# Feature work on token values kept in PSUM, in an attention and GELU kernel

## The chip, the cores and the metric

The kernel runs on one core of a Trainium2 chip. A core has TensorE (matrix products, PE in the profile, with its weight loads as PEld), VectorE (DVE), ScalarE (ACT), GpSimd (POOL) and SyncE (SP, which here only issues transfers). SBUF is the working memory, PSUM the memory that TensorE writes its products into. The metric is the device time of one execution in microseconds; before the change the median of three runs is 270.36 (270.25 to 270.38).

## What is computed

The inputs are q, k and v of 4 batches, 4 heads, 1088 tokens and 32 values each, two sketches S1 and S2 of 8 rows, and two weight matrices. In the reference, cut to what matters:

```
def phi(x):                                   # 64 features of a token
    a = einsum('rd,bhsd->bhsr', S1, x)        # 8 values
    b = einsum('rd,bhsd->bhsr', S2, x)        # 8 values
    return a (outer) b                        # 64 values
q_p, k_p = phi(q), phi(k)
kv  = k_p^T v          z = sum over tokens of k_p         # per batch and head
x   = (q_p kv) / (q_p . z + 1e-6)             # attention, 4 heads side by side: 4352 x 128
out = gelu(x @ w_in) @ w_out                  # 128 -> 2048 -> 128, exact gelu, float32
```

So every query token needs its 64 products a_i b_j, divided by its denominator, which is the sum over i, j of a_i b_j z_ij.

## The kernel before

The 4352 tokens are worked on in nine chunks: eight of 512 tokens (two for each batch, numbered 0 to 7) and one of 256 with what is left over of all batches (chunk 8). For each chunk, TensorE makes 16 hidden tiles of 128 x 512 (`hidden`, L691), ScalarE applies GELU to each (L698), GpSimd makes sums and differences of four GELU tiles at a time (`token_sums`, L741 to L744, a seven-product scheme for the second matrix), and TensorE multiplies them with w_out into two output banks (`two_products`, L776). When a chunk is done, `drain` (L788 to L797, ScalarE and VectorE) takes these two banks, `combine` (L810 to L813, VectorE) adds the parts, and `store` turns the result (L839, VectorE) and sends it out. The output banks come from a pool of two, so the next chunk's products can't begin before `drain` has read them; the buffers named "sums", which `drain` writes and `combine` and `store` read, are two as well. Chunks 0 and 1 do half of their second product in the plain way, and have one more addition in `combine` (L813).

Around this stands the attention of later chunks, on the same engines. For chunk n: `query_turn` transposes q in blocks (L535), `query_sketch` (L584) multiplies it on TensorE with a small matrix `S_abc` and leaves 16 values for each token and head in a pair of PSUM banks, a's half (4 values), c's half (4) and b (8). c is the sketch of z, folded into `S_abc`, so that the denominator is the sum of a_i c_i. `query_outer` then does everything on VectorE: it transposes the pair of banks into the SBUF tile `tok` in blocks of 32 x 32 (L595), so that a token lies in a partition, multiplies a and c (L599), sums within a partition (L601) and across to the neighbouring block of partitions, which holds the other half (L603, four instructions), adds both (L605), adds 1e-6 (L606), inverts (L607), multiplies a by it (L608), makes the outer product with b (L610, 1024 values a partition) and transposes back (L613) into `q_pT`. `attend` (L627) multiplies `q_pT` with the batch's kv on TensorE, and ScalarE copies the result to `xT` (L631), the input of `hidden`.

For keys, `finish_keys` sums kv and z of a batch on TensorE into one PSUM bank (`kv_sum`, L446: kv in columns 0 to 63, z in 64 to 127) and ScalarE copies it to `kv_T` (L470). One step later `turn_kv` turns kv on TensorE into the same bank (L475), ScalarE copies it to `kz` (L476), and `sketch_of_z` on VectorE multiplies z by the sketch (L499), reduces (L501) and writes the c part of `S_abc` (L502), which the next `query_sketch` needs. The PSUM pool `wps` has two buffers of two banks each, in turn for all of these.

The order of the work on each engine is that of the program's text: a list of steps t (one hidden tile each) with calls put at written-out steps, and a dependency from each instruction to the one before it on its engine. So an instruction that waits holds up all behind it on its engine. At step t = 32, `query_outer` of chunk 3 is written ahead of `store` of chunk 0 (t = 35) and `drain` of chunk 1 (t = 38).

Of the kernel before, what the change touches and what calls it, by code (L numbers as in the profile page):

```python
# [8 lines left out]
FP = mybir.dt.float32  # L9
U32 = mybir.dt.uint32  # L10
AX = mybir.AluOpType
# [5 lines left out]
def kernel(  # L17
# [18 lines left out]
    pe, dve, act, pool, sp = nc.tensor, nc.vector, nc.scalar, nc.gpsimd, nc.sync  # L36
    B, H, S, D = q.shape
    R = S1.shape[0]
    F = R * R
# [3 lines left out]
    NP = H // 2  # L43
# [4 lines left out]
    CW = JC * 128  # L48
# [12 lines left out]
    att = ctx.enter_context(tc.tile_pool(name="att", bufs=2))  # L61
# [5 lines left out]
    def work_banks():  # L67

        return wps.tile([128, 2, CW], FP, name="w_ps")

    def work_bank():
        return work_banks()[:, 0]
# [7 lines left out]
    def out_bank():  # L80
        return ops.tile([128, CW], FP, name="o_ps")
# [133 lines left out]
    ident = big.tile([128, 128], FP, name="ident")  # L215
# [8 lines left out]
    kz = [big.tile([128, 128], FP, name=f"kz{b}") for b in range(B)]  # L224
# [81 lines left out]
    sT = big.tile([128, 2 * R], FP, name="sT")  # L306
# [119 lines left out]
    def flat(features):  # L426
        return features.rearrange("p i j -> p (i j)")
# [16 lines left out]
    def kv_product(ps, lhsT, features, h, part, start=False, stop=False):  # L444

        pe.matmul(ps[h * D:(h + 1) * D, part * F:(part + 1) * F], lhsT=lhsT, rhs=features, start=start, stop=stop,  # L446
                  skip_group_check=True)

    def kv_sum(b, ps):


        for i in range(J):
            ch, t, one = i % 2, i // 4, i // 2 % 2
            for h in range(H):
                kv_product(ps, main["v", b][:, h, i, :], flat(k_p[b, h % 2][:, t, h // 2 * 4 + ch * 2 + one]), h, 0,
                           start=i == 0)
        for h in range(H):
            kv_product(ps, v_rem_aug[b][:, h, :], flat(k_p_rem[b % 2][:, h]), h, 0, stop=True)
        if b == 1:
            for h in range(H):  # L460
                kv_product(ps, ones_rem, flat(k_p_rem[b][:, h]), h, 1)
        for m in range(2 if b == 1 else 1):
            for h in range(H):
                kv_product(ps, ones, k_s[h % 2][:, h // 2, 0, m], h, 1, stop=b > 1 or m == 1)

    kv_T = {}

    def take_kv(b, ps):
        kv_T[b] = att.tile([128, 128], FP, name="kv_T")
        act.copy(out=kv_T[b], in_=ps[:, :128])  # L470

    def turn_kv(b, ps):

        for rows in (slice(0, 64), slice(64, 128)):
            pe.matmul(ps[rows, :128], lhsT=kv_T[b][:, :F], rhs=ident, start=True, stop=True)  # L475
        act.copy(out=kz[b], in_=ps[:, :128])  # L476
        sketch_of_z(b, kv_T[b][:, F:])


    S_abc = [big.tile([128, 2, 2, 2 * R], FP, name=f"S_abc{b}") for b in range(B)]  # L480
# [12 lines left out]
        for b in range(1, B):  # L493
            pool.tensor_copy(out=S_abc[b], in_=w)

    def sketch_of_z(b, z):

        zs = att.tile([128, R, R], FP, name="z_s")
        dve.tensor_mul(out=zs, in0=z.rearrange("p (i j) -> p i j", i=R), in1=sT[:, None, R:].broadcast_to([128, R, R]))  # L499
        c = att.tile([128, R], FP, name="c_s")  # L500
        dve.tensor_reduce(out=c, in_=zs, axis=mybir.AxisListType.X, op=AX.add)  # L501
        dve.tensor_mul(out=S_abc[b][:, :, :, 4:8], in0=c.rearrange("p (i f) -> p i f", i=2)[:, :, None].broadcast_to([128, 2, 2, 4]),  # L502
                       in1=own_r[:, None, :, None].broadcast_to([128, 2, 2, 4]))
# [11 lines left out]
    def turn_first_kv():  # L515

        ps, zs = work_bank(), held["zs"]
        for h in range(H):
            c, r = h // 2, h % 2
            pe.matmul(ps[h * D:(h + 1) * D, :F], lhsT=zs[:, r], rhs=ident[:, c * F:(c + 1) * F], start=True, stop=True)  # L520
        sketch_of_z(0, ps[:, :F])


    qT, qp, xT = {}, {}, {}
# [46 lines left out]
    sketched = {}  # L571
# [18 lines left out]
    def query_outer(n):  # L590

        W = width[n]
        K = W // 16
        tok = att.tile([128, 2, CW // 2], FP, name="A_sb").rearrange("p i x -> p (i x)")
        dve.transpose(out=tok[:, :W].rearrange("p (c x) -> p c x", c=NP), in_=sketched.pop(n)[:, :, :W // 2])  # L595
        x = tok[:, :W].rearrange("p (k x) -> p k x", x=2 * R)
        a, c, b = x[:, :, 0:4], x[:, :, 4:8], x[:, :, 8:16]
        m = att.tile([128, 32, 4], FP, name="q_ac")[:, :K]
        dve.tensor_mul(out=m, in0=a, in1=c)  # L599
        part, other = (att.tile([128, 32], FP, name=f"q_den{i}")[:, :K] for i in range(2))  # L600
        dve.tensor_reduce(out=part, in_=m, axis=mybir.AxisListType.X, op=AX.add)  # L601
        for g in range(4):
            dve.tensor_reduce(out=other[(g ^ 1) * 32:((g ^ 1) + 1) * 32], in_=m[g * 32:(g + 1) * 32], axis=mybir.AxisListType.X,  # L603
                              op=AX.add)
        dve.tensor_add(out=part, in0=part, in1=other)  # L605
        dve.tensor_scalar(out=part, in0=part, scalar1=1e-6, scalar2=None, op0=AX.add)  # L606
        dve.reciprocal(out=part, in_=part)  # L607
        dve.tensor_mul(out=m, in0=a, in1=part[:, :, None].broadcast_to([128, K, 4]))  # L608
        feat = att.tile([128, 2 * CW], FP, name="q_f", bufs=1)[:, :2 * W]
        dve.tensor_mul(out=feat.rearrange("p (k i j) -> p k i j", i=4, j=R), in0=m[:, :, :, None].broadcast_to([128, K, 4, R]),  # L610
                       in1=b[:, :, None, :].broadcast_to([128, K, 4, R]))
        qp[n] = att.tile([128, 2, CW], FP, name="q_pT")
        dve.transpose(out=qp[n].rearrange("f r x -> f (r x)")[:, :2 * W], in_=feat)  # L613

    def attend(n):
# [259 lines left out]
    banks = [out_bank(), out_bank()]  # L875
# [86 lines left out]
    held = {}  # L962
# [6 lines left out]
        key_features_rem(pair, held["rem"])  # L969

    def finish_keys(b):
        held["kv"] = work_bank()
        kv_sum(b, held["kv"])
        take_kv(b, held["kv"])

    def round_at(t, w, product_by=dve):
        r = []
# [18 lines left out]
    at(18, channel_sums, 4)  # L996

    at(21, finish_keys, 1)
    at(22, lambda: turn_kv(1, held["kv"]))
    at(23, query_turn, 3)  # L1000
    at(23, query_sketch, 2)
    at(23, query_outer, 2)
    at(29, attend, 2)
    for i, t in enumerate((25, 26, 28)):
        at(t, channel_sums, i)
    at(11, spread_sketches)
    at(40, repeat_first_z)
    at(46, turn_first_kv)
    for n in range(3, NCHUNK):

        t = (n - 1) * NF
        b = (n + 1) // 2
        keys = n % 2 and b < B
        if n > 3:
            at(t - 6, query_turn, n)
        at(t, query_sketch, n)
        at(t, query_outer, n)
        if keys:
            for r in range(2):
                at(t - 2, key_turn_blocks, b, r)  # L1020

        at(t + 7, attend, n)
        if keys:
            at(t + 5 + (n == NCH + 1), features_of_all, b)
            at(t + 5 + (n == NCH + 1), outer_of_all, b)
            at(t + 6, add_last, b, dve)
            at(t + 8, widen_v_rem, b)
            at(t + 14, finish_keys, b)
            at(t + 15, lambda b=b: turn_kv(b, held["kv"]))
# [5 lines left out]
    for t, (n, fi) in enumerate(steps):  # L1035
# [13 lines left out]
        elif fi % NB == NB - 1:  # L1049
            b = fi // NB  # L1050
# [11 lines left out]
    for t in range(len(steps) + LAG):  # L1062
        if t < 4:
# [9 lines left out]
            if t == 3:  # L1073
                banks = work_banks()
# [17 lines left out]
        if t < len(steps):  # L1092
            n, fi = steps[t]
            hidden(n, fi, by_halves=t >= 18 and (n < NMAIN or fi < 5))
        if t < len(steps) and steps[t][0] < NMAIN and steps[t][1] % NB == NB - 1:
            n, b = steps[t][0], steps[t][1] // NB
# [50 lines left out]
```

## Time and profile before

| what | us |
|---|---|
| median of 3 runs | 270.36 |
| span of the profiled run | 270.7 |
| TensorE busy | 262.9 (97%) |
| GpSimd busy | 177.9 (66%) |
| VectorE busy | 158.4 (58%) |
| ScalarE busy | 118.0 (44%) |

VectorE's groups that the diff touches, by line, with the mean of the full-width instructions and, from the timelines, the shortest and longest of those looked at:

| line | what | count | mean ns | from, to us |
|---|---|---|---|---|
| L595 | transpose out of PSUM | 6 | 709 | 0.67, 0.72 |
| L599 | a times c | 6 | 709 | 0.29, 1.27 |
| L605 | add both halves | 6 | 448 | 0.19, 0.96 |
| L606 | add 1e-6 | 6 | 555 | 0.18, 1.31 |
| L608 | a divided | 6 | 545 | 0.29, 1.05 |
| L610 | outer product | 6 | 1579 | 1.22, 2.36 |
| L613 | transpose back | 6 | 1245 | 1.25, 1.25 |
| L499 | z times sketch, from `kv_T` | 3 | 479 | 0.21, 0.74 |
| L502 | c part of `S_abc` | 4 | 604 | 0.17, 1.22 |

How to read it: the page gives shares over the whole span; a row of 40 digits gives the busy tenths of each fortieth of the span (6.8 us), and the row of the clock the granted TensorE clock in tenths. A timeline's line gives start and duration in us, the engine, the line of the kernel, the operation, output and inputs, and in brackets the idle time before it and what ended that. Equal instructions of very different durations, as in the last column, were held up by something while they ran.

### The profile page before, as it was taken

To read this page: it belongs to the slowest core of one execution; us is meant where nothing else is said; L and a number is where in the kernel's file an instruction comes from. 1 tells how busy PE (TensorE), PEld (TensorE's weight loads), DVE (VectorE), ACT (ScalarE), POOL (GpSimd) and SP (SyncE) were. 2 spreads that over 40 slices of the span, in tenths; PEclk is the share of its full clock that TensorE was granted. 3 is DMA by queue.
4 is the path that set the end of the run, shared out by engine and by line. 5 is a ranking of instruction groups with operands and counts; after the bars stand their busy time and mean duration, and the time that the engine had idled before them with its cause. 6 is when DMAs were issued, how large, how long until landed. Compare 5 with 4: busy or idle time off the path is not lost.

```text
span 270.7 us, 6127 instructions
## 1 busy us (share of the span) xinstructions
PE 262.9 (97%) x2489; PEld 135.7 (50%) x2489; DVE 158.4 (58%) x308; ACT 118.0 (44%) x239; POOL 177.9 (66%) x180
## 2 busy tenths in 40 slices
PE   8999999999999599999999999999999999999995
PEld 6755444355344255444445455544454444445794
DVE  2687778469599897577048992870097107600140
ACT  4464767433633333353336333353326333534431
POOL 3423006899999568597777776786879687868400
PEclk9999999999999799999999999999999999999999
DMA  6459363444300110101100002002000200020021
GB/s 202 126 151 368 89 175 63 115 120 125 86 10 2 23 19 14 27 2 22 17 2 2 1 0 41 2 1 39 2 0 2 40 2 0 2 39 0 2 32 26
DMA packets 35755, 13.50 MB, mean 50 GB/s; under 512 B 28432, under 2 KB 34320, under 8 KB 35728
## 3 DMA queue, kind: packets, MB, share of 16 engines
q1 hardware_dynamic: 35536, 13.05, 19.6%
q8 instruction: 19, 0.31, 0.5%
q10 hardware_dynamic: 192, 0.07, 0.1%
q14 instruction: 8, 0.07, 0.1%
HBM read 10.88 MB, written 2.23 MB: 48 GB/s over the span
## 4 chain that ended last, share of the span: by engine, by line
PE 69%; SPq 11%; DMA 10%; DVE 7%; issue 1%; ACT 0%; POOL 0%; DVEq 0%; ACTq 0%
PE h_ps L691 31%; PE o_ps L776 28%; SPq L108 7%; DMA v<-in_v_dram 5%; DMA block<-in_moe_w_out_dram 4%; PE w_ps L824 3%; SPq L124 1%; PE w_ps L858 1%; SPq L128 1%; PE w_ps L584 1%; PE w_ps L627 1%; PE w_ps L446 1%; SPq L177 1%; DVE q_f L610 1%; PE h_ps L326 1%
## 5 line engine op out<-in xcount | busy, mean ns | idle before, releaser
L691 PE MATMUL h_ps<-xT,w_in 128*64 128x512 f32 (+3 forms) x516 | 139.5, 580 | 0.0
L698 ACT ACTIVATE block<-h_ps 128x512 f32<-128x512 f32 (+1 forms) x128 | 73.1, 571 | 121.4 <-PE h_ps L691 120.5
L776 PE MATMUL o_ps<-block,w_out 128*64 128x256 f32 x224 | 58.7, 385 | 0.0
L691 PEld LDWEIGHTS h_ps<-xT,w_in 128*64 128x64 f32 (+1 forms) x516 | 42.5, 143 | 29.1 <-issue 10.7
L741 POOL TENSOR_TENSOR bits_low<-block 128x512 f32<-128x512 f32 x28 | 39.6, 1414 | 25.0 <-ACT block L698 24.9
L776 PEld LDWEIGHTS o_ps<-block,w_out 128*64 128x64 f32 x224 | 29.8, 138 | 36.2 <-issue 25.2
L742 POOL TENSOR_TENSOR bits_a<-block 128x512 f32<-128x512 f32 x28 | 38.0, 1358 | 11.5 <-ACT block L698 11.5
L743 POOL TENSOR_TENSOR bits_e<-bits_a,block 128x512 f32<-128x512 f32 x28 | 36.9, 1316 | 2.2
L744 POOL TENSOR_TENSOR bits_m<-block,bits_e 128x512 f32<-128x512 f32 x28 | 36.3, 1297 | 2.2
L776 PE MATMUL o_ps<-block,small 128*64 128x256 f32 x112 | 29.1, 382 | 2.7 <-DVE sums L792 2.7
L595 DVE STREAM_TRANSPOSE A_sb<-w_ps 128x512 f32<-128x512 f32 (+1 forms) x7 | 4.7, 672 | 43.4 <-PE w_ps L584 43.4
L776 PE MATMUL o_ps<-bits_a,small 128*64 128x256 f32 x112 | 29.6, 388 | 0.0
L776 PE MATMUL o_ps<-bits_m,w_out 128*64 128x256 f32 x112 | 29.0, 382 | 0.0
L776 PE MATMUL o_ps<-bits_low,small 128*64 128x256 f32 x112 | 29.0, 382 | 0.0
L776 PEld LDWEIGHTS o_ps<-block,small 128*64 128x64 f32 x112 | 14.8, 137 | 22.6 <-issue 11.3
L792 DVE TENSOR_TENSOR sums<-o_ps,sums 64x512 f32<-64x512 f32 x8 | 5.5, 683 | 31.5 <-ACT sums L789 23.0
L776 PE MATMUL o_ps<-bits_e,small 128*64 128x256 f32 x112 | 17.3, 388 | 0.0
L827 PE MATMUL o_ps<-g,w_out 128*128 128x512 f32 x32 | 16.4, 599 | 0.1
L776 PEld LDWEIGHTS o_ps<-bits_a,small 128*64 128x64 f32 x112 | 15.0, 139 | 0.0
L776 PEld LDWEIGHTS o_ps<-bits_m,w_out 128*64 128x64 f32 x112 | 14.8, 137 | 0.0
L776 PEld LDWEIGHTS o_ps<-bits_low,small 128*64 128x64 f32 x112 | 14.8, 137 | 0.0
L776 PEld LDWEIGHTS o_ps<-bits_e,small 128*64 128x64 f32 x112 | 7.9, 138 | 11.3 <-issue 9.4
(187 smaller groups left out, 322.3 us busy)
## 6 DMA issues: line engine op xcount, KB each, us to landing
block<-in_moe_w_in_dram SPq DMA_DIRECT2D x3, 512.0 KB, 7.0
block<-in_moe_w_out_dram SPq DMA_DIRECT2D x3, 512.0 KB, 11.0
k<-in_k_dram SPq DMA_DIRECT2D x48, 32.0 KB, 1.8
v<-in_v_dram SPq DMA_DIRECT2D x3, 512.0 KB, 4.3
q<-in_q_dram SPq DMA_DIRECT2D x24, 64.0 KB, 3.3
out_dram<-oT SPq DMA_DIRECT2D x24, 64.0 KB, 2.2
k<-in_k_dram SPq DMA_DIRECT2D x2, 256.0 KB, 2.9
q<-in_q_dram SPq DMA_DIRECT2D x2, 256.0 KB, 4.0
```

Source lines behind the costliest of these rows:

```text
L108: sp.dma_start(out=main["k", b][pb * 32:(pb + 1) * 32, h].rearrange("t (jj jc) d -> t jj (jc d)", jj=4), in_=src[h, pb])
L595: dve.transpose(out=tok[:, :W].rearrange("p (c x) -> p c x", c=NP), in_=sketched.pop(n)[:, :, :W // 2])
L691: pe.matmul(ps[rows, :W], lhsT=w[:, rows], rhs=xT[n][:, :W], start=True, stop=True)
L698: act.activation(out=g_of[n, fi][:, :W], in_=ps[:, :W], func=ACT.Gelu)
L741: pool.tensor_sub(out=s[3], in0=a11, in1=a21)
L742: pool.tensor_add(out=s[1], in0=a21, in1=a22)
L743: pool.tensor_sub(out=s[2], in0=s[1], in1=a11)
L744: pool.tensor_sub(out=s[4], in0=a12, in1=s[2])
L776: pe.matmul(acc[n][bank][half * 64:(half + 1) * 64, col:col + HW], lhsT=fixed, rhs=moving, start=opens and e == 0 and name in "4715", stop ...
L792: dve.tensor_add(out=C[lo, 1], in0=a1[lo], in1=C[lo, 0])
L824: pe.matmul(o_of[n][i][:, :128], lhsT=g[:, i * 128:(i + 1) * 128], rhs=w_tile(w_out_sb, fi), start=first, stop=final)
L827: pe.matmul(o_of[n], lhsT=w_tile(w_out_sb, fi), rhs=g, start=first, stop=final)
```

## The change

The values of a token are no longer copied to SBUF: the transpose writes into the free halves of the same pair of PSUM banks, and a, b, c are read from there. c is copied to SBUF first, since it is multiplied with a. The two additions for the denominator become one instruction with one PSUM and one SBUF input. The outer product is two instructions, one for each bank. In `turn_kv` the pair's second bank takes the turned kv, z is read from the first bank instead of `kv_T`, and the reduced c stays in PSUM. The aim is that none of VectorE's operations in the feature work reads two operands from SBUF, the memory that GpSimd works on at the same time.

```diff
-    def turn_kv(b, ps):
+    def turn_kv(b, banks):
 
         for rows in (slice(0, 64), slice(64, 128)):
-            pe.matmul(ps[rows, :128], lhsT=kv_T[b][:, :F], rhs=ident, start=True, stop=True)
-        act.copy(out=kz[b], in_=ps[:, :128])
-        sketch_of_z(b, kv_T[b][:, F:])
+            pe.matmul(banks[rows, 1, :128], lhsT=kv_T[b][:, :F], rhs=ident, start=True, stop=True)
+        act.copy(out=kz[b], in_=banks[:, 1, :128])
+        sketch_of_z(b, banks[:, 0], F)
...
-    def sketch_of_z(b, z):
+    def sketch_of_z(b, ps, at):
 
         zs = att.tile([128, R, R], FP, name="z_s")
-        dve.tensor_mul(out=zs, in0=z.rearrange("p (i j) -> p i j", i=R), in1=sT[:, None, R:].broadcast_to([128, R, R]))
-        c = att.tile([128, R], FP, name="c_s")
+        dve.tensor_mul(out=zs, in0=ps[:, at:at + F].rearrange("p (i j) -> p i j", i=R), in1=sT[:, None, R:].broadcast_to([128, R, R]))
+        c = ps[:, 2 * F:2 * F + R]
         dve.tensor_reduce(out=c, in_=zs, axis=mybir.AxisListType.X, op=AX.add)
...
-        sketch_of_z(0, ps[:, :F])
+        sketch_of_z(0, ps, 0)
...
     def query_outer(n):
 
         W = width[n]
-        K = W // 16
-        tok = att.tile([128, 2, CW // 2], FP, name="A_sb").rearrange("p i x -> p (i x)")
-        dve.transpose(out=tok[:, :W].rearrange("p (c x) -> p c x", c=NP), in_=sketched.pop(n)[:, :, :W // 2])
-        x = tok[:, :W].rearrange("p (k x) -> p k x", x=2 * R)
-        a, c, b = x[:, :, 0:4], x[:, :, 4:8], x[:, :, 8:16]
+        K, H2 = W // 16, W // 2
+        ps = sketched.pop(n)
+        tok = ps[:, :, CW // 2:CW // 2 + H2]
+        dve.transpose(out=tok, in_=ps[:, :, :H2])
+        x = tok.rearrange("p c (k x) -> p c k x", x=2 * R)
+        a, b = x[:, :, :, 0:4], x[:, :, :, 8:16]
         m = att.tile([128, 32, 4], FP, name="q_ac")[:, :K]
-        dve.tensor_mul(out=m, in0=a, in1=c)
-        part, other = (att.tile([128, 32], FP, name=f"q_den{i}")[:, :K] for i in range(2))
+        den = att.tile([128, 32], FP, name="q_den")[:, :K]
+        by_c = lambda t: t.rearrange("p (c k) i -> p c k i", c=NP)
+        dve.tensor_copy(out=by_c(m), in_=x[:, :, :, 4:8])
+        dve.tensor_mul(out=by_c(m), in0=a, in1=by_c(m))
+        part = ps[:, 0, :K]
         dve.tensor_reduce(out=part, in_=m, axis=mybir.AxisListType.X, op=AX.add)
         for g in range(4):
-            dve.tensor_reduce(out=other[(g ^ 1) * 32:((g ^ 1) + 1) * 32], in_=m[g * 32:(g + 1) * 32], axis=mybir.AxisListType.X,
+            dve.tensor_reduce(out=den[(g ^ 1) * 32:((g ^ 1) + 1) * 32], in_=m[g * 32:(g + 1) * 32], axis=mybir.AxisListType.X,
                               op=AX.add)
-        dve.tensor_add(out=part, in0=part, in1=other)
-        dve.tensor_scalar(out=part, in0=part, scalar1=1e-6, scalar2=None, op0=AX.add)
-        dve.reciprocal(out=part, in_=part)
-        dve.tensor_mul(out=m, in0=a, in1=part[:, :, None].broadcast_to([128, K, 4]))
+        dve.scalar_tensor_tensor(out=den, in0=part, scalar=1e-6, in1=den, op0=AX.add, op1=AX.add)
+        dve.reciprocal(out=den, in_=den)
+        dve.tensor_mul(out=by_c(m), in0=a,
+                       in1=den.rearrange("p (c k) -> p c k", c=NP)[:, :, :, None].broadcast_to([128, NP, K // 2, 4]))
         feat = att.tile([128, 2 * CW], FP, name="q_f", bufs=1)[:, :2 * W]
-        dve.tensor_mul(out=feat.rearrange("p (k i j) -> p k i j", i=4, j=R), in0=m[:, :, :, None].broadcast_to([128, K, 4, R]),
-                       in1=b[:, :, None, :].broadcast_to([128, K, 4, R]))
         qp[n] = att.tile([128, 2, CW], FP, name="q_pT")
+        for c in range(NP):
+            dve.tensor_mul(out=feat[:, c * W:(c + 1) * W].rearrange("p (k i j) -> p k i j", i=4, j=R),
+                           in0=by_c(m)[:, c, :, :, None].broadcast_to([128, K // 2, 4, R]),
+                           in1=b[:, c, :, None, :].broadcast_to([128, K // 2, 4, R]))
         dve.transpose(out=qp[n].rearrange("f r x -> f (r x)")[:, :2 * W], in_=feat)
...
     def finish_keys(b):
-        held["kv"] = work_bank()
-        kv_sum(b, held["kv"])
-        take_kv(b, held["kv"])
+        held["kv"] = work_banks()
+        kv_sum(b, held["kv"][:, 0])
+        take_kv(b, held["kv"][:, 0])
```

## The prediction, made before the changed kernel ran

> **What bounds the kernel now.** I read the page first (shares, then the 40 slices), then busy time in stretches of 5 us, then the timelines of the one stretch that fell out. TensorE is the bound nearly everywhere:
>
> ```profile
> PE 262.9 (97%) x2489; PEld 135.7 (50%) x2489; DVE 158.4 (58%) x308; ACT 118.0 (44%) x239; POOL 177.9 (66%) x180
> PE   8999999999999599999999999999999999999995
> PEclk9999999999999799999999999999999999999999
> ```
>
> TensorE is idle for 270.7 - 262.9 = 7.8 us. The first 25 us and the drain of the last outputs are not touched by the change. In between there is one hole, the slice with "5", and it lies where the granted clock reads "7". The stretches (PE, PE load, DVE, ACT, POOL busy, then the clock) say the same:
>
> ```profile
> 85.00:90.00 5.00, 3.31 (x88) 1.40 (x84) 4.72 (x5) 0.69 (x2) 3.36 (x3) 1.00 0.00 0
> 90.00:95.00 5.00, 3.97 (x20) 1.89 (x22) 4.50 (x9) 2.72 (x10) 3.70 (x3) 0.70 0.21 31
> ```
>
> VectorE is busy for 4.7 and 4.5 of 5 us there. TensorE's timeline gives the hole to 10 ns, and VectorE's and ScalarE's give its cause:
>
> ```profile
> 87.65 0.66 PE L627 MATMUL w_ps<-q_pT,kz 64*32 64x256 f32 x16
> 91.03 0.43 PE L776 MATMUL o_ps<-block,small 128*64 128x256 f32 x1 [2.72 <-DVE sums L792]
> ```
>
> ```profile
> 75.83 0.67 DVE L595 STREAM_TRANSPOSE A_sb<-w_ps 128x512 f32<-128x512 f32 x1
> ...
> 78.34 0.96 DVE L605 TENSOR_TENSOR q_den<-q_den,q_den 128x32 f32<-128x32 f32 x1
> 79.34 1.31 DVE L606 TENSOR_SCALAR q_den<-q_den 128x32 f32<-128x32 f32 x1
> 80.68 0.35 DVE L607 RECIPROCAL q_den<-q_den 128x32 f32<-128x32 f32 x1
> 81.07 1.05 DVE L608 TENSOR_TENSOR q_ac<-A_sb,q_den 128x128 f32<-128x128 f32 x1
> 82.15 2.21 DVE L610 TENSOR_TENSOR q_f<-q_ac,A_sb 128x1024 f32<-128x1024 f32 x1
> 84.40 1.25 DVE L613 STREAM_TRANSPOSE q_pT<-q_f 128x1024 f32<-128x1024 f32 x1
> ...
> 89.09 0.71 DVE L839 STREAM_TRANSPOSE oT<-sums 128x512 f32<-128x512 f32 x1
> 90.30 0.68 DVE L792 TENSOR_TENSOR sums<-o_ps,sums 64x512 f32<-64x512 f32 x1 [0.49 <-ACT sums L789]
> ```
>
> ```profile
> 89.90 0.37 ACT L789 COPY sums<-o_ps 64x256 f32<-64x256 f32 x1 [1.87 <-DVE oT L839]
> ```
>
> Read it backwards. The next accumulation (L776) needs bank a1, free when L792 has read it; L792 waits for ScalarE's L789; L789 overwrites a "sums" buffer and waits for L839; L839 stands in VectorE's queue behind query_outer of chunk 3 (75.83 to 85.65) and the combine of chunk 0 (L810 to L813). So here VectorE's queue sets TensorE's time, and query_outer is 9.8 us of it. Elsewhere TensorE goes back to back, and a faster VectorE is worth nothing.
>
> The hole costs more than its 2.72 us. From 91.03 to 95.79 TensorE did sixteen products in eight pairs, four single ones (bits_e) and one hidden tile: 0.87 + 0.87 + 0.44 + 0.85 = 3.03 us by the same groups at 80.7 to 82.9. It took 4.76, and starts were 0.42 us apart instead of 0.21. So about 1.6 us of slow clock hang on the hole (0.1 I leave to restart). Together 2.72 + 1.6 = 4.3 us.
>
> [...] L605, L606, L608 took 0.96, 1.31, 1.05 us here while GpSimd ran token sums, and 0.19, 0.18, 0.29 in chunk 4 (from 114.14 us), where it paused. L606 from 79.34 to 80.65 spans GpSimd's L743, 79.33 to 80.61. [...] Here the transpose from PSUM (L595, 709 ns) is 7 ns dearer than that from SBUF (L535, 702). [...]
>
> **The change, part by part.**
> (a) query_outer. The token tile lies in PSUM, so the first product, the division product and the outer product read one PSUM and one SBUF operand. Cost from quiet rows: transpose 0.70; added copy 0.29 (as a 128x128 product); product 0.29; reduce 0.29; four reduces 1.15; one scalar-tensor-tensor for L605 and L606 0.20; reciprocal 0.35; product 0.29; outer product in two, 0.68 + 0.62 (L958, half PSUM, four in 2.46); transpose 1.25. Sum 6.1, with eleven starts at 0.03: 6.4 us. Writing PSUM from VectorE is not in the trace: [...] I take 6.7[...]. Against 9.82 in this stage that is 3.1 us less. Over seven chunks the five groups fall from 25.5 to about 16.5 us of VectorE time, all but this stage hidden behind TensorE.
> (b) Then L810, L811, L813 (two SBUF inputs, unchanged) and L839 took 4.2 us; they meet GpSimd again, so I keep it. query_outer ends at 82.5, L839 at 86.7, L789 at 87.1, L792 at 87.9, its last follower L797 2.3 later at 90.2. TensorE comes to L776 at 88.31 and to bank a0 (for L797) 0.87 + 0.44 + 0.86 later, at 90.5. So both are in time, with 0.4 and 0.3 us to spare: the hole and the slow clock go, -4.3 us.
> (c) turn_kv. z is read from PSUM, and the sketch's reduce and product write and read PSUM. That frees three small operations of GpSimd (z_s 0.74 to 0.23, S_abc 0.85 to about 0.2 at 56 us). But the built streams show that z_s now waits two ScalarE instructions later: not for the copy of kv_T (L470) but for that of kz (L476), since both banks are one tile. At batch 1:
>
> ```profile
> 56.13 0.74 DVE L499 TENSOR_TENSOR z_s<-kv_T,sT 128x64 f32<-128x64 f32 x1 [5.17 <-ACT kv_T L470]
> ```
>
> ```profile
> 57.32 0.26 ACT L476 COPY kz<-w_ps 128x128 f32<-128x128 f32 x1
> ```
>
> ```profile
> 58.13 0.67 PE L584 MATMUL w_ps<-qT,S_abc 64*32 64x256 f32 x16 [0.28 <-DVE S_abc L502]
> ```
>
> Queued behind z_s on VectorE are only its own reduce and product and the next transpose of q; the one who waits is TensorE's L584, with everything behind it. New time: kz ends 57.58, plus 0.06, z_s 0.23, reduce 0.22, product 0.20, starts 0.06, signal 0.05: 58.40, against 58.13: +0.27. At batch 2 kz ends at 109.90, so L584 may go at 110.72 instead of 110.54: +0.18. At batch 3, 167.48 and 168.12: +0.18. [...] Sum +0.6, TensorE time with nothing to hide it.
> (d) The pair of work banks is held through query_outer and the sketch instead of being free after the first transpose. With two pairs in turn the next owner of that pair is the chunk after the coming attend, and attend waits for the same query_outer anyway: nothing. The GpSimd instructions that VectorE held up become shorter (L742 at 83.24 took 2.28 against 1.30): hidden, nothing waits for them.
>
> Sum: 270.36 - 4.3 + 0.6 = 266.7; a small remainder of (b), 0.1 on average: 266.8.
>
> **Rivals.**
> 1. The chain in (b) stays a little late. For: the spare is 0.3 to 0.4[...]. Against: the 4.2 us taken already holds two such meetings. With 0.3 to 1.2 us of hole left and no slow clock, 267.1 to 268.0: say 267.6.
> 2. The waits of (c) cost nothing and the slow clock hides still more: 266.1. Against: ScalarE's kz copy ends only 0.6 us before L584, and three operations don't fit in that.
> 3. VectorE's queue is no shorter, since the PSUM forms are dear (0.4 us each on eight, which eats the 3.1)[...]. The hole stays and (c) adds 0.6: 271.0, slower. [...] Against: L958, L792 and L499 with one PSUM operand run at 0.68, 0.68 and 0.23 us, as fast as SBUF.
> 4. The hole is half closed and the slow clock stays: 270.36 - 1.36 + 0.6 = 269.6.
>
> **How the numbers follow.** Forecast 58%, rival 1 20%, rival 2 10%, rival 3 6%, rival 4 6% (a third of it within 0.2%). The time is the likeliest: 266.8. The range takes in rivals 1 and 2 and the bounds of (a) and (c): 265.8 to 268.2. Faster by over 0.2% (below 269.8): 0.92; same 0.02; slower 0.06.
>
> **What would show it.** Right: no digit under 9 in the PE and clock rows between 60 and 250 us; VectorE's operations of query_outer alike in all chunks of full width, 6.4 to 6.9 us in sum; L776 after the attend of chunk 3 with no wait; z_s released by L476, and L584 after it 0.2 to 0.3 us late three times. Wrong: a hole left near 88 us, a copy or product on PSUM well over 0.4 us, or a new hole where attend waits for q_pT.

## The result, and the profile after

The changed kernel takes 266.67 us (266.58 to 266.76, four runs) against 270.35 before (four runs on the same chip): a ratio of 0.9865, with a 95% interval of 0.9848 to 0.9882. The forecast was 266.8 us.

The page of the changed kernel has no hole left, and the clock's row is even:

```profile
PE 258.7 (98%) x2489; PEld 133.4 (50%) x2489; DVE 146.7 (55%) x315; ACT 118.0 (45%) x239; POOL 170.2 (64%) x180
...
PE   8999999999999999999999999999999999999995
...
PEclk9999999999999999999999999999999999999999
```

VectorE lost 11.7 us of busy time and GpSimd, whose code is untouched, 7.7. The same two stretches as before (PE, PE load, DVE, ACT, POOL busy, clock), and TensorE's timeline at the place of the hole:

```profile
85.00:90.00 5.00, 5.00 (x46) 2.01 (x44) 4.31 (x10) 3.59 (x12) 3.36 (x3) 1.00 0.20 31
90.00:95.00 5.00, 5.00 (x40) 2.61 (x38) 4.90 (x8) 1.22 (x3) 3.82 (x6) 1.00 0.17 26
```

```profile
85.75 0.66 PE L633 MATMUL w_ps<-q_pT,kz 64*32 64x256 f32 x16
86.37 0.43 PE L782 MATMUL o_ps<-block,small 128*64 128x256 f32 x1
```

L782 (L776 before) now follows the attend at once. VectorE's queue in the same stage (start, duration):

```profile
74.19 0.68 DVE L596 STREAM_TRANSPOSE w_ps<-w_ps 128x512 f32<-128x512 f32 x1
...
77.05 0.19 DVE L609 SCALAR_TENSOR_TENSOR q_den<-w_ps,q_den 128x32 f32<-128x32 f32 x1
77.28 0.35 DVE L610 RECIPROCAL q_den<-q_den 128x32 f32<-128x32 f32 x1
77.66 0.29 DVE L611 TENSOR_TENSOR q_ac<-w_ps,q_den 128x128 f32<-128x128 f32 x1
77.99 1.29 DVE L616 TENSOR_TENSOR q_f<-q_ac,w_ps 128x512 f32<-128x512 f32 x2
79.31 1.25 DVE L619 STREAM_TRANSPOSE q_pT<-q_f 128x1024 f32<-128x1024 f32 x1
80.48 0.81 DVE L816 TENSOR_TENSOR sums<-sums 64x256 f32<-64x256 f32 x1
81.30 1.41 DVE L817 TENSOR_TENSOR sums<-sums 64x256 f32<-64x256 f32 x1
82.75 1.65 DVE L819 TENSOR_TENSOR sums<-sums,g 128x512 f32<-128x512 f32 x1
84.43 0.71 DVE L845 STREAM_TRANSPOSE oT<-sums 128x512 f32<-128x512 f32 x1
85.63 0.68 DVE L798 TENSOR_TENSOR sums<-o_ps,sums 64x512 f32<-64x512 f32 x1 [0.49 <-ACT sums L795]
```

query_outer takes 6.37 us (74.19 to 80.56) where it took 9.82. But the reader should see the last line too: L798 ends at 86.31, and TensorE comes for its bank at 86.37. The spare time is 0.06 us; the combine (L816 to L819), with two SBUF inputs each, takes 3.9 us where it took 3.5 before:

```profile
85.56 0.38 DVE L810 TENSOR_TENSOR sums<-sums 64x256 f32<-64x256 f32 x1
85.95 1.40 DVE L811 TENSOR_TENSOR sums<-sums 64x256 f32<-64x256 f32 x1
87.39 1.67 DVE L813 TENSOR_TENSOR sums<-sums,g 128x512 f32<-128x512 f32 x1
```

The wait that the change adds, on VectorE and on TensorE (0.28 us before, 0.58 now):

```profile
55.66 0.23 DVE L499 TENSOR_TENSOR z_s<-w_ps,sT 128x64 f32<-128x64 f32 x1 [6.64 <-ACT kz L476]
```

```profile
56.48 0.67 PE L584 MATMUL w_ps<-qT,S_abc 64*32 64x256 f32 x16 [0.58 <-DVE S_abc L502]
```

Where the time went can be read by laying TensorE's marks of both traces side by side. The profiled run of the kernel before has a time of 272.47, and in its first 10 us the same groups of TensorE took up to 1.8 times as long as after (L550, 32 products: 1.99 us against 1.12), though the row of the clock is even there. So I count from the kv sum of batch 1 (54.22 before, 52.27 after):

| mark on TensorE | after minus before, us | step |
|---|---|---|
| query_sketch of chunk 2 | +0.30 | waits for S_abc |
| query_sketch of chunk 3 | +0.06 | 0.24 regained |
| kv sum of batch 2 | -4.25 | hole and slow clock, 4.3 |
| query_sketch of chunk 4 | -4.02 | +0.23, waits for S_abc |
| query_sketch of chunk 6 | -3.86 | +0.15 from -4.01 just ahead, waits for S_abc |
| attend of chunk 8 | -3.84 | |

### The profile page after: what moved, and what is told of

Read it like the earlier page. It is cut to its first block, busy times and chain, and to the rows that moved or that the text cites. A ratio compares the mean times of both kernels' runs of the same rounds, so it can differ in the third digit from the quotient of the medians.

```text
span 264.9 us, 6135 instructions
## 1 busy us (share of the span) xinstructions
PE 258.7 (98%) x2489; PEld 133.4 (50%) x2489; DVE 146.7 (55%) x315; ACT 118.0 (45%) x239; POOL 170.2 (64%) x180
## 4 chain that ended last, share of the span: by engine, by line
PE 93%; DVE 2%; DMA 2%; ACT 1%; issue 1%; SPq 0%; POOL 0%; DVEq 0%
PE h_ps L697 43%; PE o_ps L782 33%; PE o_ps L833 5%; PE w_ps L830 3%; DMA q<-in_q_dram 2%; PE w_ps L584 2%; PE w_ps L633 1%; PE w_ps L446 1%; PE w_ps L368 1%; ACT block L704 1%; PE o_ps L435 0%; PE h_ps L712 0%; PE w_ps L550 0%; PE w_ps L649 0%; DVE x_tok L670 0%
## 5 line engine op out<-in xcount | busy, mean ns | idle before, releaser
L782 PE MATMUL o_ps<-block,w_out 128*64 128x256 f32 x224 | 58.2, 382 | 0.0
L747 POOL TENSOR_TENSOR bits_low<-block 128x512 f32<-128x512 f32 x28 | 36.0, 1286 | 25.5 <-ACT block L704 25.5
L782 PEld LDWEIGHTS o_ps<-block,w_out 128*64 128x64 f32 x224 | 29.4, 137 | 35.5 <-issue 24.2
L748 POOL TENSOR_TENSOR bits_a<-block 128x512 f32<-128x512 f32 x28 | 35.8, 1277 | 14.7 <-ACT block L704 14.7
L749 POOL TENSOR_TENSOR bits_e<-bits_a,block 128x512 f32<-128x512 f32 x28 | 36.3, 1297 | 2.2
L782 PE MATMUL o_ps<-bits_a,small 128*64 128x256 f32 x112 | 29.2, 383 | 0.0
L782 PE MATMUL o_ps<-bits_low,small 128*64 128x256 f32 x112 | 29.0, 382 | 0.0
L782 PE MATMUL o_ps<-bits_m,w_out 128*64 128x256 f32 x112 | 29.0, 382 | 0.0
L782 PE MATMUL o_ps<-block,small 128*64 128x256 f32 x112 | 29.0, 382 | 0.0
L596 DVE STREAM_TRANSPOSE w_ps<-w_ps 128x512 f32<-128x512 f32 (+1 forms) x7 | 4.8, 686 | 40.8 <-PE w_ps L584 40.7
L798 DVE TENSOR_TENSOR sums<-o_ps,sums 64x512 f32<-64x512 f32 x8 | 5.5, 683 | 37.6 <-ACT sums L795 26.4
L782 PEld LDWEIGHTS o_ps<-block,small 128*64 128x64 f32 x112 | 14.8, 137 | 19.8 <-issue 11.3
L782 PE MATMUL o_ps<-bits_e,small 128*64 128x256 f32 x112 | 16.8, 379 | 0.0
L782 PEld LDWEIGHTS o_ps<-bits_m,w_out 128*64 128x64 f32 x112 | 14.8, 137 | 0.0
L782 PEld LDWEIGHTS o_ps<-bits_low,small 128*64 128x64 f32 x112 | 14.8, 137 | 0.0
L782 PEld LDWEIGHTS o_ps<-bits_a,small 128*64 128x64 f32 x112 | 14.6, 137 | 0.0
L782 PEld LDWEIGHTS o_ps<-bits_e,small 128*64 128x64 f32 x112 | 8.0, 137 | 11.0 <-issue 9.4
```

The source lines that it names most:

```text
L596: dve.transpose(out=tok, in_=ps[:, :, :H2])
L747: pool.tensor_sub(out=s[3], in0=a11, in1=a21)
L748: pool.tensor_add(out=s[1], in0=a21, in1=a22)
L749: pool.tensor_sub(out=s[2], in0=s[1], in1=a11)
L782: pe.matmul(acc[n][bank][half * 64:(half + 1) * 64, col:col + HW], lhsT=fixed, rhs=moving, start=opens and e == 0 and name in "4715", stop ...
L798: dve.tensor_add(out=C[lo, 1], in0=a1[lo], in1=C[lo, 0])
```

## The experiments

Theory: all gain comes from one stage, query_outer of chunk 3, whose two-input operations wait for GpSimd; the keys' part only costs. Rivals: every chunk has its share; or the instructions are faster for another reason.

**One half of the change each.** First query_outer alone, with the keys' functions as before; then these alone:

```diff
-        sketch_of_z(b, banks[:, 0], F)
+        sketch_of_z(b, kv_T[b][:, F:])      # and finish_keys, c_s, turn_first_kv as before
```

> query_outer as in the changed kernel, keys (turn_kv, sketch_of_z, finish_keys) as before. Theory (the hole at chunk 3 pays, the later z_s costs): the hole and its slow clock go (-4.3 us) and the three added waits at query_sketch, 0.30 + 0.23 + 0.14 in the trace of the changed kernel, go too: 266.0 us. Rival (the keys' part helps as well, by freeing GpSimd): above 266.7. Rival (the added waits are hidden behind something else): 266.7.

Measured 266.77 us, ratio 0.9892 (0.9868 to 0.9916). Its waits of TensorE for other engines:

```profile
PE o_ps L782 <- DVE sums L798: 0.5, 1, 0.5
...
PE w_ps L584 <- DVE S_abc L502: 0.2, 1, 0.2
```

The three added waits are gone, and yet the time is no better than with them. TensorE comes 0.33 us earlier to the stage of chunk 3 (sketch of chunk 3 at -0.27 instead of +0.06), and VectorE starts query_outer that much earlier too; but its combine ends no earlier, and 0.5 us of hole opens there:

```profile
79.99 1.37 DVE L816 TENSOR_TENSOR sums<-sums 64x256 f32<-64x256 f32 x1
```

L816 took 0.81 us in the changed kernel. The engine that is late is GpSimd. It ends its sums of this stage 31.81 us after the start of the kv sum of batch 1 (83.93), against 31.58 in the changed kernel, where it goes from one operation to the next all that time. So the stall of TensorE ahead of the place where GpSimd is late cost nothing here; it moved from L584 (0.58 us in the changed kernel, 0.24 here) to L782 (0.52 here). The rival that the keys' part frees GpSimd has a small share in it: by these two traces GpSimd is 0.2 us later without that part.

> Keys' part of the change alone, query_outer as before. Theory: three waits of TensorE for S_abc, 0.67 us in sum, and the hole stays: 271.0 us. Rival (fewer two-input operations help GpSimd and so the whole): below 270.3.

Measured 270.63 us, ratio 1.0018 (0.9995 to 1.0041): by the ratio some 0.5 us over the kernel before on this chip (269.29), not to be told from zero. The trace has the waits for S_abc, 0.7 us in sum, and the hole:

```profile
PE   8999999999999799999999999999999999999995
PEclk9999999999999999999999999999999999999999
...
PE o_ps L776 <- DVE sums L792: 2.3, 1, 2.3
```

Here is a surprise: a hole of 2.3 us, and the clock stays whole. The mean granted clock was recorded for every execution: it is 1.0 in 11 of these 22, and 0.994 in the other 11. With like clocks compared, the keys' part costs 0.37 us (medians 269.52 against 269.15 at 1.0) and 0.25 (270.73 against 270.48 below it).

**One chunk alone.** The new query_outer for chunk 3 only, and for all others (keys as before):

```diff
+    def query_outer(n):
+        (query_outer_psum if n == 3 else query_outer_sbuf)(n)      # the second kernel: n != 3
```

> The new query_outer for chunk 3 alone; the other six chunks and the keys as before. Theory (only the stage of chunk 3 is bounded by VectorE): the whole gain, 266.0 to 266.1 us, as with all seven. Rival (each chunk has its share of the gain): some 0.6 us of it, 269.7.

Measured 266.36 us, ratio 0.9881 (0.9858 to 0.9904); the attend of chunk 8 stands at -4.18. One of seven chunks brings the whole gain. The rival of equal shares is out.

> The new query_outer for all chunks but chunk 3; keys as before. Theory: hole and slow clock stay, so 270.3 us, although VectorE loses some 8 us of busy time. Rival (each chunk has its share): 266.7 to 267.

Measured 267.95 us, ratio 0.9933 (0.991 to 0.9955). This I had wrong: without any change to chunk 3 a part of the gain is there. VectorE in the stage of chunk 3:

```profile
76.39 1.03 DVE L605 TENSOR_TENSOR q_den<-q_den,q_den 128x32 f32<-128x32 f32 x1
77.46 1.31 DVE L606 TENSOR_SCALAR q_den<-q_den 128x32 f32<-128x32 f32 x1
...
85.45 0.69 DVE L847 TENSOR_TENSOR sums<-sums,g 128x512 f32<-128x512 f32 x1
```

L605 and L606 are as slow as before. But L847, the combine's last addition (L813 before, 1.67 us there), meets no GpSimd: that was not held up in chunk 2's query_outer, and is done with its sums at 85.13. The hole is 2.0 us instead of 2.72, the clock is whole in all six executions (0.998 to 1.0), and 0.28 us is regained ahead (the mark of the table's second row stands at -0.28). Beside the executions of the kernel before with a whole clock on this chip (median 269.15) that is a gain of 1.2 us, beside the others (270.48) one of 2.5. By the marks it arises before the kv sum of batch 2 (-2.51 there, -2.49 at the attend of chunk 8), so the other six chunks, too, gain only at this stage and just ahead of it.

**GpSimd without reads.** The kernel before, VectorE's code untouched:

```diff
-        pool.tensor_sub(out=s[3], in0=a11, in1=a21)
...
+        for j in (3, 1, 2, 4):
+            for i in range(2):
+                pool.memset(s[j], 0.125 * j)
```

> The kernel before, with GpSimd's token sums left out: each is replaced by two memsets of the same tile, so GpSimd writes SBUF and reads nothing there, and the output isn't the reference's. VectorE's instructions are untouched. Theory (two-input operations wait for GpSimd's reads): q_ac, q_den and q_f operations with two SBUF inputs run at their quiet durations (0.29, 0.19, 0.29, 1.22 us) in every chunk, the hole closes: 265.8 us. The addition of 1e-6 (one input, SBUF to SBUF) may still meet GpSimd's writes: up to 0.6 us. Rival (they are slow for another reason, such as their operands or the waits between them): durations as before, 270.4 us.

Measured 265.33 us, ratio 0.9838 (0.9805 to 0.9872). VectorE (L809, L810 and L812 are the combine, L810, L811 and L813 before):

```profile
75.82 0.19 DVE L605 TENSOR_TENSOR q_den<-q_den,q_den 128x32 f32<-128x32 f32 x1
76.04 0.48 DVE L606 TENSOR_SCALAR q_den<-q_den 128x32 f32<-128x32 f32 x1
...
76.95 0.29 DVE L608 TENSOR_TENSOR q_ac<-A_sb,q_den 128x128 f32<-128x128 f32 x1
77.28 1.22 DVE L610 TENSOR_TENSOR q_f<-q_ac,A_sb 128x1024 f32<-128x1024 f32 x1
...
79.70 0.37 DVE L809 TENSOR_TENSOR sums<-sums 64x256 f32<-64x256 f32 x1
80.09 0.42 DVE L810 TENSOR_TENSOR sums<-sums 64x256 f32<-64x256 f32 x1
80.55 0.69 DVE L812 TENSOR_TENSOR sums<-sums,g 128x512 f32<-128x512 f32 x1
```

The same instructions, operands and waits run at their quiet durations once GpSimd only writes (L605 0.19 us against 0.96, L608 0.29 against 1.05, L610 1.22 against 2.21), in the combine as well (L810 and L812 0.42 and 0.69 against 1.40 and 1.67); so in this stage it is the token sums, which read SBUF, that hold up those with two SBUF inputs, and not writes alone. L606, with one input and SBUF on both sides, still takes 0.48 us against 0.18 while memsets run (75.39 to 76.50). (A pair of memsets takes GpSimd 1.10 to 1.14 us here, the sum that it replaces 1.30 to 1.41 on average, so a little of the gain may be that.)

**How late may VectorE be?** Four and eight idle reduces ahead of the combine:

```diff
+        if n == 0:
+            spare = att.tile([128, 32], FP, name="q_spare")
+            for i in range(4):
+                dve.tensor_reduce(out=spare, in_=ones[:, :, None].broadcast_to([128, 32, 4]), axis=mybir.AxisListType.X, op=AX.add)
         C, N = drained.pop(n)
```

> The changed kernel with four idle reduces of 0.29 us (no two SBUF inputs) put in VectorE's queue ahead of the combine of chunk 0. Theory (hole of TensorE = lateness of VectorE's queue, spare time 0.06 us): a hole of about 1.1 us near 86 us. If the clock holds through a hole of this length: 267.8 us. If any hole drops it: about 269.4.

> The same with eight reduces: VectorE 2.35 us later. Theory: a hole of about 2.3 us; 269.0 us if the clock holds, 270.6 if it falls as it did after the 2.7 us of the kernel before. Rival (the hole isn't set by this queue): 266.7.

Measured 267.28 us, ratio 0.9897 (0.9869 to 0.9926), and 267.86 us, ratio 0.9927 (0.9905 to 0.9949): holes of 0.4 and 0.7 us, not 1.1 and 2.3. With eight reduces:

```profile
80.83 2.49 DVE L817 TENSOR_REDUCE q_spare<-ones 128x32 f32<-128x128 f32 x8
83.24 1.11 DVE L820 TENSOR_TENSOR sums<-sums 64x256 f32<-64x256 f32 x1
84.36 0.42 DVE L821 TENSOR_TENSOR sums<-sums 64x256 f32<-64x256 f32 x1
84.82 0.69 DVE L823 TENSOR_TENSOR sums<-sums,g 128x512 f32<-128x512 f32 x1
```

Counted in both traces from the start of query_outer of chunk 3 (74.55 here, 74.19 in the changed kernel), the queue starts its combine 2.40 us later, and ends it (L823 against L819) only 0.75 later. With four reduces it is 1.12 and 0.40. Less the spare 0.06 us that is 0.34 and 0.69, and the holes are 0.35 and 0.71. The queue had been waiting for GpSimd's last two sums anyway, which end at 83.85 in the changed kernel:

```profile
81.09 1.34 POOL L749 TENSOR_TENSOR bits_e<-bits_a,block 128x512 f32<-128x512 f32 x1
82.51 1.34 POOL L750 TENSOR_TENSOR bits_m<-block,bits_e 128x512 f32<-128x512 f32 x1
```

So the hole is the lateness of the queue's end less the spare time, as I thought, but a delay ahead of the combine does not pass to that end in full: the three two-input operations of the combine meet the sums, and their end hangs on when GpSimd is through. With eight reduces its sums end at 84.07, and L821 and L823 behind that take 0.42 and 0.69 us, where L817 and L819 took 1.41 and 1.65. Of the eight-reduce kernel four of 14 executions lay above 269 us. The recorded clock is 1.0 in all of them, so it was not that; what it was stays open.

**Orders that do better.** The sketch of z ahead of the copy to kz, and then also the store of chunk 0 ahead of query_outer of chunk 3:

```diff
+        sketch_of_z(b, banks[:, 0], F)
         act.copy(out=kz[b], in_=banks[:, 1, :128])
-        sketch_of_z(b, banks[:, 0], F)
```

> The changed kernel with one order changed: in turn_kv the sketch of z stands ahead of ScalarE's copy to kz, so that z_s waits for TensorE's turned kv and the kz copy waits for the sketch. Theory (z_s waits too long for the kz copy): z_s starts 0.6 us earlier, no wait of TensorE for S_abc is left, also not the 0.28 us that the kernel before had at chunk 2: 265.7 us. Rival (the PSUM forms themselves are slow, or the kz copy now delays the GELU tiles behind it): 266.5 or above.

Measured 266.2 us, ratio 0.9859 (0.9834 to 0.9884). No wait for S_abc is left, but 0.4 us of hole comes back at L782, as in the kernel with query_outer alone; by the marks it gains 0.49 us on the changed kernel, not 0.95. TensorE reaches the stage 0.5 us earlier (sketch of chunk 3 at -0.44), but GpSimd ends its sums 31.52 us after the start of the kv sum of batch 1, nearly as late as there (31.58).

```diff
-                done[t + 12].append(n)
+                done[t + (8 if n == 0 else 12)].append(n)
```

> The changed kernel with the sketch of z ahead of the kz copy (as in the run before with that order) and, new, with the store of chunk 0 four steps earlier, so that its combine stands ahead of query_outer of chunk 3 in VectorE's queue and not between it and the drain. Theory (with no waits for S_abc left, what remains is the combine, held up by GpSimd, between query_outer and the drain: 0.4 us of hole): drain no longer waits for it, q_pT comes 0.2 us ahead of attend; no hole: 265.8 us, 0.4 under the order without it. Rival (q_pT late, attend waits instead): 266.2 or above.

> The changed kernel as it is, on the same chip as the run beside it, to compare the two and to see how far its times spread. Theory: no hole, so no slow clock that comes and goes: times within 0.5 us of each other at 266.7, while the kernel before spreads over some 2 us in two groups about 1.4 us apart (with and without the slow clock after its hole).

Measured 265.86 us (265.38 to 266.10), ratio 0.9841 (0.9809 to 0.9874), beside the changed kernel's 266.81 (266.50 to 266.99), ratio 0.9876 (0.984 to 0.9911). The six times of the one lie all under the six of the other. The drain now follows query_outer at once:

```profile
84.17 1.25 DVE L619 STREAM_TRANSPOSE q_pT<-q_f 128x1024 f32<-128x1024 f32 x1
85.34 0.64 DVE L798 TENSOR_TENSOR sums<-o_ps,sums 64x512 f32<-64x512 f32 x1
```

The attend of chunk 3 starts at 85.76, 0.34 after q_pT. This version beats both kernels: all waits of TensorE between the first 20 us and the last are gone, and the attend of chunk 8 stands at -4.94 (-4.33 with the earlier sketch alone). The earlier store was not run by itself.

## Why the prediction was right

**The bound and its place.** Right. One hole, set by VectorE's queue, and query_outer of chunk 3 in it: that chunk alone gives the whole gain (266.36 us).

**The 4.3 us.** Right for the run it was read from: the marks give 4.31. But 1.6 of it is the slow clock, and it isn't always there. Of 59 executions of the kernel before on three chips, 27 have a recorded mean clock of 1.0, and these are the 27 between 268.77 and 269.56 us; 32 have 0.991 to 0.994, and these are all the others, from 270.16 upward. On each chip the medians of the two groups lie 1.2 to 1.5 us apart, and a mean of 0.994 over 268 us is 1.6 us of clock lost, as much as the traced hole cost. On the chip that ran both kernels side by side, the changed one (266.81, clock 0.999 to 1.0) gains 2.4 us on the first group and 3.9 on the second. So a ratio also says how its base was mixed. For the four executions behind 270.35 no clock was recorded; by their times, and by the 0.991 of the profiled execution, they belong to the second group. That the gain came out at 3.7 us and not at 2.4 is to that extent luck: the prediction took the slow clock from one trace and for certain. What decides between the groups no run shows.

**(a) query_outer.** 6.37 us; the quiet rows had given 6.4, and the 0.3 us that I laid on for PSUM were not needed. They, and the 6.9 us that I allowed at most, were my estimate; no trace had shown them. The product and the copy out of PSUM take 292 ns, as two SBUF operands do when quiet; the reduce into PSUM 295 against 286, the transpose into PSUM 723 against 709.

**(b) the combine "took 4.2 us; they meet GpSimd again, so I keep it".** This term was mis-sized. From L816 to the end of L845 it is 4.66 us. With (a) shorter by 0.3, this longer by 0.5 and TensorE 0.24 us sooner by (d), the spare time was 0.06 us, not 0.4: rival 1 missed by a hair. For bank a0 nothing was left: L803 ends at 88.63, and TensorE took 0.96 us from its hidden tile at 87.72 to the next product at 88.68, where the tile at 79.71 took 0.86. That is as much as the remainder of 0.1 us in the sum. The delays and the run without GpSimd's reads show what stands in place of a fixed 4.2 us: 2.2 us of work, and waits that end with GpSimd's sums.

**(c) the later z_s.** Right in kind and size: 0.30, 0.23 and 0.15 us against 0.27, 0.18 and 0.18. The trace has z_s released by L476, as forecast. That both banks being one tile is the reason was not tested by itself; the two instructions touch different banks, and with the sketch written first the wait is gone. What I did not see is that the first of them, 0.30 us ahead of the hole's place, was nearly free: without it a hole of 0.5 us opens, and the kernel with query_outer alone takes as long (266.77).

**(d) "hidden, nothing waits for them".** Wrong by 0.24 us, in our favour. In the kernel before, a channel sum of GpSimd met VectorE's L610 of chunk 2 (66.24 to 67.47), took 1.30 us where its like took 0.32 at 68.56, and the sums behind it came late:

```profile
66.35 1.30 POOL L729 TENSOR_TENSOR small<-w_out 128x64 f32<-128x64 f32 x1
...
72.15 1.29 POOL L743 TENSOR_TENSOR bits_e<-bits_a,block 128x512 f32<-128x512 f32 x1
```

```profile
73.49 0.65 PE L776 MATMUL o_ps<-bits_e,small 128*64 128x256 f32 x4
```

TensorE's pairs of products start 0.21 us apart, the last at 73.08, so it could have gone on at 73.29; it did at 73.49, when L743 had ended at 73.44. After the change the same L729 (L735) takes 0.33 us and TensorE does not stop. It cancels most of the first wait of (c).

So the forecast of 266.8 us held with three small errors: 0.3 too much for PSUM, 0.5 too little for the combine, 0.24 not counted. That they left 0.06 us of spare time and not a hole is luck. The time did not hang on it: query_outer alone has a hole of 0.5 us and lacks the waits of (c), and takes 266.77.

## What to carry to other kernels

When instructions of one form have very different durations, look at what the other engine that works on the same memory does in the same microseconds (L605 took 0.96 us beside GpSimd's token sums and 0.19 without), and then whether any of it lies where the bound engine waits: here one chunk's saving brought everything, and that of the other six a part, at the same stage and just ahead of it. A stall of 0.30 us just ahead of a place where another engine was late cost nothing here, and taking it away brought nothing while the later place was as it was (266.77 us against 266.67); count spare time there before you sum up gains. If a queue is late once, see whether a call that has time (here a store) can be moved out from between: together with the earlier sketch it took away the hole that faster instructions had left.

## What the runs showed of the hardware

An operand in PSUM cost VectorE little or nothing: 292 ns for 128 x 128 out of PSUM against 0.29 us out of SBUF, 9 ns more for the reduce into PSUM (295 against 286) and 14 for the transpose (723 against 709). Two-input operations on SBUF that GpSimd's token sums had stretched to 0.96 and 1.05 us (L605, L608) took 0.19 and 0.29 in the run with its memsets, which only write.

TensorE's mean clock fell below 0.995 in some executions of one and the same kernel and not in others: in 32 of 59 of the kernel before, whose traced execution has a hole of 2.7 us, and in 11 of 22 of the keys' part alone, with a traced hole of 2.3; in none of six with a hole of 2.0, and in none of 14 with one of 0.7. In the traced execution of the kernel before, it fell not in the hole but at 92 us, 1 us after TensorE had gone on (91.03): the granted clock was 1.00 from 90 to 91.5, 0.99 from 91.5 to 92, 0.50 from 92 to 95, 0.59 from 95 to 95.5 and 1.00 after that, which makes about 3.4 us at half.

A delay of 2.4 us in VectorE's queue moved its end by 0.75 us, since the operations behind it had been waiting for GpSimd.
